# Block 2's dense 2: a third group of four w2 tiles in seven products

## The chip, the core and the metric

The kernel runs on one core of a Trainium2 chip. The metric is the device time of one execution in microseconds (us); the median of three runs is given for the kernel before. The engines are TensorE (PE, matmuls), VectorE (DVE), ScalarE (ACT), GpSimd (POOL, used here mostly to issue DMAs) and SyncE (SP, which issues DMAs in order).

## The reference

Two layers on the same input x of 2048 rows x 1024 columns are added to x. The first is a state space layer on the layer-normed x, a complex linear recurrence over the rows with 1024 states; the second is a dense layer (1024 to 3584), the Mish activation and a second dense layer (3584 to 1024), on the layer-normed x too:

```python
Lam_bar = jnp.exp(dt * Lam)
B_bar = ((Lam_bar - 1.0) / Lam)[:, None] * Bmat
Bu = jnp.einsum("bld,pd->blp", x + 0j, B_bar)
for t in range(L):
    h = Lam_bar[None, :] * h + Bu[:, t, :]
y = 2.0 * jnp.einsum("blp,dp->bld", hseq, Cmat).real + x * Dskip[None, None, :]

h = jnp.einsum("bsd,df->bsf", x, w1) + b1
sp = jnp.log1p(jnp.exp(-jnp.abs(h))) + jnp.where(h > 0, h, 0)
return jnp.einsum("bsf,fd->bsd", h * jnp.tanh(sp), w2)

xn = _layernorm(x)
return x + A(xn) + B(xn)
```

## The kernel before

The 2048 rows are worked in four blocks of 512. A block's work has two halves. The first is the projections: w1 (dense 1) and the B matrix, whose results are activated (Mish) or rotated into the recurrence's frame. The second, in `tail`, adds up dense 2 (w2) and the C product of the states in the eight PSUM banks, one bank for each of 4 row quarters x 2 column halves. While PE does dense 2, DVE runs the recurrence (`recur`, one call for each of eight state tiles j), and each block ends with four `finish` operations that add PSUM and the kept sums into the output rows. Block 3's projections follow block 2's last matmul directly.

From block 1 on many products are done in seven matrix products for eight (Strassen's scheme in Winograd's form). For dense 2 this works on groups of four K tiles of w2: two tiles from the first 14 and two from the last 14, each cut into column halves. The seven products take four raw or summed weights and activations: products 1, 2 and 4 use raw activations, and 7, 5, 6 and 3 use sums that DVE makes (`act_sums`). The weight side of a group is made once: `d2_load` brings four raw tiles on POOL, or `d2_row` takes them from the ring, in both cases ACT scales them, three raw units are stored to a DRAM area `w2d` and four differences (`d2_sums`, each a `step` with one DVE operation and one POOL store) are made in place and stored. The steps wait in a list `later` and are run by `some(n)`, or by a `k0` in the written-out order of a block's projections.

`NFG` says how many groups each block does so: 2 of 7 in block 2, all 7 in block 3. What block 2 does not do in seven products is its list `PLAIN`: pairs of w2 tiles straight from the input, 16 matmuls a pair (`dense`). While such a pair lies in the ring, ACT also scales the raw tiles of the groups named in `PASSING` from it, for block 3. `SCALED_AT` says which activation tiles ACT scales behind which pair.

Weights come through a ring of seven slots of 512 KB (`ring`, `items`, `ring_load`, `ring_fill`): `ws` are w1 units, `tp` units of w2d (two a slot), `w2` plain pairs, `c` the C matrix, `ts` block 3's w2d. SP issues the loads in that order, and each load waits until PE (and ACT, where it reads the slot) is done with the slot's former content.

The order of the work is written out by hand in strings: `STEPS` for block 2's projections, `LAST` for block 3's. Letters p q s w x y z are w1 products, a to d those of B, `G` is `act_scale` of two activation tiles, `g` Mish, `u` block 2's first dense-2 products, `t` `act_sums`, `I` ring slots given back, `h` and `m` raw w2 tiles, `k` a step. In `dense_part` (block 2) come: products 1, 7, 2, 5, 6 with their `keep` (PSUM to the buffer KS), then the plain list, then products 3 and 4. After it come the C products of six state tiles, and by row quarter those of the last two, with `finish` behind each. `carry` and `uncarry` are seven small DVE operations that take the recurrence's last state to the next block.

Of the kernel before, what the change touches and what calls it, by code (L numbers as in the profile page):

```python
# [163 lines left out]
def build_kernel(nc, A_x, A_Lambda_re, A_Lambda_im, A_B_re, A_B_im, A_C_re, A_C_im,  # L164
# [11 lines left out]
    GF = 7  # L176
# [8 lines left out]
    TILES = [*range(12)]  # L185
    NFG = {2: 2, 3: GF}
    W2_ORDER = (*range(9), 13, *range(9, 13))
    EARLY, LATE = ((0, 18), (26, 28)), ((18, 26),)
    PLAIN = [(f, f + 1) for f in (4, 18, 6, 20, 24, 10, 8, 22, 12, 26)]
    PASSING = {4: 2, 18: 2, 6: 3, 20: 3, 8: 4, 22: 4}  # L190
    SCALED_AT = {4: (20,), 18: (24,), 6: (10,), 20: (8, 22), 10: (12,), 8: (26,)}
    WHOLE = ("a2 a1 V0 b2 b1 a5 b5 V1 P4 P5 a6 b6 v6 P6 P7 a3 b3 P0 a7 b7 P1 Q0 n0 p1 q1 a4 b4 "
# [3 lines left out]
    STEPS = ("p1 p5 p2 q1 q5 p6 q2 s1 k0 p7 s5 p3 k0 q6 s2 p4 k0 q7 q3 k0 s6 q4 m1 k0 g0 a2 a1 k0 s7 s3 b2 b1 k0 s4 g1 k0 a5 "  # L196
             "b5 a6 b6 a3 h4 b3 S0 a7 h5 b7 c2 d2 h6 a4 b4 h7 l0 c5 c1 d5 d1 r0 c6 G0 c3 G1 d6 d3 c7 G2 w1 d7 r1 w5 w2 G3 c4 d4 k0 E0 E1 w6 x1 x5 x2 k0 w7 k0 w3 r2 "
             "x6 w4 k0 y1 y5 y2 x7 x3 E2 E3 y6 x4 z1 z5 g2 z2 y7 y3 z6 G7 y4 z3 z7 u0 t0 G8 u2 z4 I1 u1 t1 t2")
    LAST = ("p1 p5 p2 q1 q5 p6 q2 s1 p7 s5 p3 q6 s2 M5 p4 q7 q3 k0 k0 s6 q4 g0 a2 a1 k0 s7 k0 s3 O0 O0 O0 O0 m6 b2 b1 s4 G1 G0 g1 a5 G3 b5 G2 a6 b6 "
# [213 lines left out]
    for blk in range(NB):  # L413
        items += W_ITEMS if blk in SPLIT else O_ITEMS if blk == FAST else [("w1", g) for g in range(NF // 2)]
        if blk == NB - 1:
            items += [("ts", m) for m in range((NT + 3) // 4)]
        elif blk in SPLIT:
            units = [("tp", 7 * p + i) for p in range(7) for i in range(0, NFG[blk], 2)]
            items += units[:5 * NFG[blk] // 2] + [("w2", (4 * REAL[f // 4] + f % 4) // 2) for f, _ in PLAIN] + units[5 * NFG[blk] // 2:]
        else:  # L420
            items += [("w2", g) for g in W2_ORDER]
        items += [("c", j) for j in range(NJ)] if blk >= FAST else []
    n_loaded = [0]

    def ring_load():
        i = n_loaded[0]
        if i >= len(items):
            return
        n_loaded[0] += 1
        kind, g = items[i]  # L430
        s = i % NRING
        if kind == "w1":

            dst = ring[:, s, :].rearrange("p (k f) -> p k f", k=NK // 2)
            r0 = (g % 2) * D // 2
            src = B_w1[r0:r0 + D // 2, (g // 2) * 512:(g // 2 + 1) * 512].rearrange("(k p) f -> p k f", p=P)
        elif kind == "w2":
            dst = ring[:, s, :].rearrange("p (f d) -> p f d", f=2)
            src = B_w2[g * 256:(g + 1) * 256, :].rearrange("(f p) d -> p f d", p=P)
        else:  # L440
            dst, src = ring[:, s, :], ctd[g] if kind == "c" else None
            if kind == "ts":
                n = min(4, NT - 4 * g) * TB
                dst, src = ring[:, s, 0:n], w2d[g][:, 0:n]
        s_ring[s].nper = len(g) if kind == "ws" else 2 if kind == "tp" else 1
        if kind == "tp":
            for h in range(2):
                src = w2d[(g + h) // 2][:, (g + h) % 2 * 1024:((g + h) % 2 + 1) * 1024]
                SP.dma(lambda e, h=h, src=src: e.dma_start(ring[:, s, h * 1024:(h + 1) * 1024], src),
                       s_ring[s], reads=[b_w2d[g + h]], writes=[b_ring[s].parts[h]])  # L450
            return
        if kind == "ws":
            for h, (i, n) in enumerate(g):
                SP.dma(lambda e, h=h, i=i, n=n: e.dma_start(ring[:, s, h * 1024:(h + 1) * 1024], wsd[i][n - 1]),
                       s_ring[s], reads=[b_wsd[i][n - 1]], writes=[b_ring[s].parts[h]])
            return
        SP.dma(lambda e: e.dma_start(dst, src), s_ring[s], reads=[b_ctd[g]] if kind == "c" else b_w2d[2 * g:2 * g + 2] if kind == "ts" else [],
               writes=[b_ring[s]])
# [396 lines left out]
    def ring_fill():  # L855
        while n_loaded[0] < min(n_item[0] + NRING, len(items)):
            kind, g = items[n_loaded[0]]
            need = [b_wsd[i][n - 1] for i, n in g] if kind == "ws" else b_w2d[2 * g:2 * g + 2] if kind == "ts" else b_w2d[g:g + 2] if kind == "tp" else []
            if any(b.writer is None for b in need):
                return  # L860
            ring_load()
# [339 lines left out]
    KIND = (1, 7, 2, 5, 6, 3, 4)  # L1201
    D2_RAW = [((k, t), (k, t + 4)) for k, t in (("h", 8), ("h", 0), ("s", 0))]
    D2_RAW += [(("a", 20), ("a", 6)), (("a", 24), ("a", 10)), (("h", 0), ("h", 4)), (("h", 8), ("h", 12))]
    spare = {"h": (hb, b_hbf), "a": (act, b_actf), "s": (CT[:, :, 1, TB:D], [b for s in b_snap for b in s.parts])}
# [39 lines left out]
    def d2_sums(g):  # L1244
        (lo, b_lo), (hi, b_hi) = d2_half(g, 0), d2_half(g, 1)
        b11, b12, b21, b22 = ((v[:, :, d, :], b[d::2]) for v, b in ((lo, b_lo), (hi, b_hi)) for d in range(2))
        sem = DmaSem(nc, "d_ts%d" % g, nper=4)
        f = lambda u: (u[0].bitcast(f16), u[1])
        for n, o, x, y, h, d in ((5, b11, b12, b11, 0, 0), (7, b12, b22, b12, 0, 1), (6, b22, b22, f(b11), 1, 1),
                                 (4, b21, b21, f(b22), 1, 0)):  # L1250
            def step(n=n, o=o, x=x, y=y, h=h, d=d):
                vop(lambda e: e.tensor_tensor(o[0].bitcast(f16), x[0], y[0], op=ALU.subtract),
                    reads=x[1] + y[1], writes=o[1])
                d2_store(g, n, h, d, sem)

# [57 lines left out]

    CHUNKS = {2: ((0, 4),), 3: ((0, 6), (6, 12), (12, 14))}
    b_SA = [[Buf("SA%d_%d" % (n, i)) for i in range(3)] for n in range(4)]
# [43 lines left out]
    def project_fast(blk, order, open_unit):  # L1359
        keep = {}  # L1360
        for o in order.split():
# [38 lines left out]
            elif kind == "Q":  # L1400
                row_powers(EARLY)
            elif kind == "O":
                held.pop(0)(SP)
# [80 lines left out]
    def tail(blk, base):  # L1484
# [46 lines left out]
        def fast(n, i, k):  # L1531
# [3 lines left out]
            p, ng = KIND.index(n), 2 * NFG[blk]  # L1535
            at = p * ng + k + (4 * len(PLAIN) if near and p >= 5 else 0)
            s = (base + at // 4) % NRING
# [7 lines left out]
            else:  # L1545
# [5 lines left out]
                  reads=b_t + [b_ring[s]], writes=[b_ps[bank]], first=begin, last=end, chained=begin and not st_,  # L1551
                  tell=i == 1 and (at % 4 == 3 or at == NT - 1))

# [22 lines left out]
        def dense_part():  # L1576
# [9 lines left out]
            for k in range(ng):  # L1586
                fast(2, 1, k)
            for _ in range(ng // 2):
                item_done()
            for n in KIND[3:]:  # L1590
                for k in range(ng):
                    for i in range(2):
                        fast(n, i, k)
                    if k % 4 == 3:
                        item_done()
# [4 lines left out]
                if n == 6:  # L1600
                    keep(3, BANKS[6])
                    act_scale(blk, 9)
                    plain_root()
# [95 lines left out]
        ends = blk == NB - 1  # L1699
        if blk in SPLIT:  # L1700
            for m, q0, h in ((0, 0, 0), (1, 0, 1), (2, 2, 0), (3, 2, 1))[2 if near else 0:]:
                b_x = [b_xx[i][q].parts[h] for q in (q0, q0 + 1)]
                vop(lambda e, m=m, q0=q0, h=h: e.tensor_tensor(
                    KS[:, m, :, :], KS[:, m, :, :], xx[:, i, q0:q0 + 2, h * TB:(h + 1) * TB], op=ALU.add),
                    reads=[b_KS[m]] + b_x, writes=[b_KS[m]])
        if ends:
            tmp, b_tmp = KS[:, 3, 1, :], b_KS[3]
            vop(lambda e: e.scalar_tensor_tensor(out=tmp, in0=ps[:, 7, :], scalar=wz[:, 3:4], in1=tmp, op0=ALU.mult, op1=ALU.add),
                reads=[b_ps[7], b_tmp, b_wz[3]], writes=[b_tmp])
        for q in range(NQ):  # L1710
            units = (2 * q, 2 * q + 1) if not (ends and q == NQ - 1) else (2 * q,)
            for j in range(NJ - njt, NJ):
# [119 lines left out]
    for blk in range(NB):  # L1832
# [67 lines left out]
        for j in range(NJ):  # L1900
# [8 lines left out]
            if blk in SPLIT:  # L1909
                if near and j == 0:  # L1910
                    act_sums(blk, ((4, 0),))
                    next(out_stage)
                if near and j in (2, 4, 7):
                    some(4)
                if j == 6:
# [3 lines left out]
            if blk:  # L1919
# [7 lines left out]
                if j == 5:  # L1927
                    w_exponent(1)
                    row_powers(LATE)
                    row_bound()  # L1930
                    for i in range(2):
                        w_scale(i)
                continue
            if j == 0:
# [15 lines left out]
        if near:  # L1950
            for q in range(NQ):
                ln_skip(blk + 1, q)
            for n in range(4):
                sums_x(blk + 1, n)
        if 0 < blk < NB - 1:
            carry()
        if blk == SPLIT[0]:
            uncarry()
        if blk == FAST:
# [19 lines left out]
        if blk == FAST - 1:  # L1979
            w_scale(4)  # L1980

    SP.wait(out_events.values())
# [34 lines left out]
```

## Time and profile before

| | |
|---|---|
| median of 3 runs | 589.18 us (589.16 to 589.87) |
| the profiled execution | 589.72 us, of which the profile's span is 588.5 |
| PE busy | 582.6 us (99%) |
| DVE busy | 510.5 us (87%) |
| ACT busy | 400.5 us (68%) |
| DMA queue of SP and the others in hardware | 105.99 MB in the largest, 60.0% of the 16 engines' span |

The times of the profile count from the span's start. In it block 1's dense 2 starts near 230 us, block 2's projections at 307, its dense 2 at 374, its C products at 421, and block 3's projections at 449. A line number such as L1491 is a line of the kernel; L1491 is `acc`, the matmul of plain dense tiles and of C, L1550 is `fast`, the matmul of the seven products, L1023 and L947 are the projections. A bracket at the end of a timeline's row is the idle time of the engine before it and who ended it.

### The profile page before, as it was taken

Reading aid. Unit: us, or ns where it says so; the run is one execution under the profiler, and the core shown is the slowest. Engines: PE = TensorE matmul, PEld = TensorE weight load, DVE = VectorE, ACT = ScalarE, POOL = GpSimd, SP = SyncE. Lnnn points to the kernel's source line nnn. Section 1 sums busy time; section 2 is a strip of 40 time slices with the busy share of each in tenths; the row PEclk is TensorE's granted clock in tenths of the full one; section 3 lists DMA queues with packets and bytes.
Section 4 is the critical chain, followed back from the end, with each engine's and each line's share of the span. In section 5 each row is a group of like instructions: output and inputs, shape, how many; then the busy total and the mean of one; then the engine's idle time right before and its main releaser. Section 6 shows DMA issues by size and latency. Waiting matters only on the chain.

```text
span 588.5 us, 9772 instructions
## 1 busy us (share of the span) xinstructions
PE 582.6 (99%) x3606; PEld 354.2 (60%) x3643; DVE 510.5 (87%) x791; ACT 400.5 (68%) x538; POOL 149.9 (25%) x213
## 2 busy tenths in 40 slices
PE   8999999999999999999999999999999999999998
PEld 7644444444447887444458888644446888844444
DVE  6999998998997878998976869899999469789995
ACT  4869993758578878999506787899512798992330
POOL 2899300123624420441211221011410013100000
PEclk9999999999999999999999999999999999999999
DMA  9999999999688978899879858869985956989832
GB/s 254 244 257 221 212 224 227 305 338 362 183 308 287 352 239 309 296 315 258 300 234 381 293 176 299 300 227 264 341 324 176 384 200 230 331 311 329 295 113 72
DMA packets 114585, 158.48 MB, mean 269 GB/s; under 512 B 55658, under 2 KB 66538, under 8 KB 114538
## 3 DMA queue, kind: packets, MB, share of 16 engines
q1 hardware_dynamic: 97696, 105.99, 60.0%
q0 software_dynamic: 13184, 43.53, 21.4%
q10 hardware_dynamic: 3658, 8.34, 4.0%
q8 instruction: 29, 0.48, 0.3%
q14 instruction: 18, 0.15, 0.1%
HBM read 111.69 MB, written 34.08 MB: 248 GB/s over the span
## 4 chain that ended last, share of the span: by engine, by line
PE 96%; DMA 1%; ACT 1%; SPq 1%; issue 1%; DVE 0%; ACTq 0%
PE ps L1491 40%; PE ps L1023 19%; PE ps L947 12%; PE ps L870 10%; PE ps L1550 8%; PE ps L1426 5%; DMA ring<-in_B_w_dram 1%; PE ps L688 1%; ACT act L893 1%; PE ps L1514 1%; ACT act L900 1%; PE ps L679 0%; SPq L398 0%; PE ps L1522 0%; DVE act L1046 0%
## 5 line engine op out<-in xcount | busy, mean ns | idle before, releaser
L1491 PE MATMUL ps<-ring,act 128*128 128x512 bf16 x594 | 131.0, 379 | 0.7
L1491 PEld LDWEIGHTS ps<-ring,act 128*128 128x128 bf16 x608 | 59.5, 98 | 71.3
L1043 ACT ACTIVATE snaps<-ps,par,cs 128x256 f32<-128x256 f32 x98 | 53.5, 563 | 58.6 <-PE ps L1023 54.3
L1491 PE MATMUL ps<-ring,hT 128*128 128x512 bf16 x354 | 78.2, 379 | 0.4
L1023 PE MATMUL ps<-TT,ring 128*128 128x256 f16 x552 | 68.3, 273 | 0.0
L909 DVE TENSOR_TENSOR mt<-hT,tab 128x2048 bf16<-128x2048 bf16 (+1 forms) x56 | 67.9, 1212 | 0.4
L1491 PEld LDWEIGHTS ps<-ring,hT 128*128 128x128 bf16 x362 | 35.4, 98 | 42.7
L1441 DVE TENSOR_TENSOR_SCAN hT<-cs,qi,hT 128x512 bf16<-128x512 f32 x48 | 60.6, 1273 | 0.0
L1023 PEld LDWEIGHTS ps<-TT,ring 128*128 128x128 f16 (+1 forms) x552 | 53.8, 98 | 7.2 <-issue 0.2
L870 PE MATMUL ps<-xnT,ring 128*128 128x512 bf16 x258 | 56.8, 379 | 0.3
L1060 DVE SCALAR_TENSOR_TENSOR act<-ps,cs,snaps 128x512 bf16<-128x512 f32 x54 | 39.8, 747 | 19.2 <-PE ps L1023 17.1
L1023 PE MATMUL ps<-xnT,ring 128*128 128x256 bf16 x424 | 53.9, 273 | 0.0
L1222 POOL DMA_DIRECT2D w2d<-hb x28 | 20.0, 717 | 96.6 <-ACT hb L1232 52.6
L1023 PEld LDWEIGHTS ps<-xnT,ring 128*128 128x128 bf16 (+1 forms) x424 | 41.4, 98 | 5.4 <-ACT snaps L1043 0.2
L870 PEld LDWEIGHTS ps<-xnT,ring 128*128 128x128 bf16 x264 | 25.8, 98 | 31.0
L1461 ACT ACTIVATE hT<-hT,wz 128x1024 bf16<-128x1024 bf16 x16 | 17.9, 1145 | 27.4 <-DVE hT L1456 27.4
L893 ACT ACTIVATE act<-act 128x2048 bf16<-128x2048 bf16 (+3 forms) x12 | 32.8, 2756 | 4.7 <-DVE act L1046 4.7
L972 DVE TENSOR_TENSOR hT<-ps,snaps 128x512 f16<-128x512 f32 x36 | 23.8, 686 | 13.9 <-ACT snaps L964 12.6
L1172 POOL DMA_DIRECT2D wsd<-hb x35 | 18.9, 545 | 55.3 <-DVE hb L1194 31.3
L1550 PE MATMUL ps<-ring,act 128*128 128x512 bf16 (+1 forms) x129 | 29.1, 379 | 0.2
L878 ACT ACTIVATE act<-ps,par 128x512 bf16<-128x512 f32 (+1 forms) x40 | 23.6, 663 | 7.3 <-PE ps L870 7.3
L1426 PE MATMUL ps<-xnT,BT 128*128 128x512 bf16 x126 | 27.7, 379 | 0.1
(241 smaller groups left out, 1055.3 us busy)
## 6 DMA issues: line engine op xcount, KB each, us to landing
ring<-wsd SPq DMA_DIRECT2D x122, 256.0 KB, 4.6
ring<-in_B_w_dram SPq DMA_DIRECT2D x58, 512.0 KB, 5.5
ring<-ctd SPq DMA_DIRECT2D x24, 512.0 KB, 4.5
ring<-w2d SPq DMA_DIRECT2D x24, 512.0 KB, 5.4
wsd<-hb POOLq DMA_DIRECT2D x35, 256.0 KB, 4.5
w2d<-hb POOLq DMA_DIRECT2D x28, 256.0 KB, 5.0
hb<-in_B_w_dram POOLq DMA_DIRECT2D x20, 256.0 KB, 4.9
ctd<-CT ACTq DMA_DIRECT2D x8, 512.0 KB, 5.4
```

Source lines behind the costliest of these rows:

```text
L870: PE.mm(lambda e, k=k, w=w: e.matmul(ps[:, bank, :], lhsT=w, rhs=xnT[:, k, :], start=k == 0, stop=k == NK - 1), reads=[b_ring[s]] + b_xnT, ...
L893: aop(lambda e: e.activation(t, t, AF.Mish), reads=b, writes=b)
L909: vop(lambda e: e.tensor_tensor(mt[:], u.unsqueeze(1).to_broadcast([P, 2, 2, TB]), tab[:, :, j, :].unsqueeze(2).to_broadcast([P, 2, 2, TB] ...
L947: PE.mm(lambda e, w=w, x=x, o=o, begin=begin, end=end: e.matmul(ps[:, bank, o:o + TH], lhsT=w, rhs=x, start=opens and begin, stop=end, ski ...
L972: vop(lambda e: e.tensor_tensor(dst, bank(b), src, op=ALU.add), reads=[b_ps[b], b_src], writes=b_hT[ci][j0:j0 + 2])
L1023: PE.mm(lambda e, w=w, x=x, o=o, begin=begin, end=end: e.matmul(ps[:, bank, o:o + TH], lhsT=w, rhs=x, start=opens and begin, stop=end, ski ...
L1043: aop(lambda e, o=o, p=p, j=j: e.activation(o, p, AF.Identity, scale=ig, bias=b1(f0 + j)), reads=[b_ps[b], b_par, b_ig], writes=b_dst)
L1060: vop(lambda e: e.scalar_tensor_tensor(out=dst, in0=bank(b), scalar=ig, in1=src, op0=ALU.mult, op1=ALU.add), reads=[b_ps[b], b_snap[k], b_ ...
L1426: PE.mm(lambda e, j=j, ci=ci, k=k, bank=bank: e.matmul(ps[:, bank + ci, :], lhsT=BT[:, ci, j, k, :], rhs=xnT[:, k, :], start=k == 0, stop= ...
L1441: vop(lambda e: e.tensor_tensor_scan(out=hT[:, ci, j, :], data0=cj("r", j).to_broadcast([P, TB]), data1=hT[:, ci, j, :], initial=init, op0 ...
L1491: PE.mm(lambda e: e.matmul(ps[:, u, :], lhsT=lhsT, rhs=rhs, start=st_, stop=last, skip_group_check=blk in SPLIT), reads=reads, writes=[b_p ...
L1550: PE.mm(lambda e: e.matmul(ps[:, bank, :], lhsT=lhsT, rhs=rhs, start=st_, stop=end, skip_group_check=True), reads=b_t + [b_ring[s]], write ...
```

## The change

Block 2 takes a third group of four w2 tiles in seven products (`NFG` 3), and `PLAIN` loses the pairs (4, 5) and (18, 19). With three groups the first five products hold 15 units, an odd number, so their last ring slot holds one unit. The third group's raw tiles are no longer taken from the ring in block 2's plain list: `d2_load(2)` and `d2_scale(2)` bring and scale them at j = 5 of block 1's recurrence, into activation tiles 8 to 15, and four more `k0` in `STEPS` make its differences. The remaining groups' sources, the scalings in `SCALED_AT` and the places of the layer norm's steps in the plain list move up. The last difference of each group has a semaphore of its own. In block 2's `finish` part the additions of x into the kept sums 2 and 3 come after the second `finish`, not before the first; `carry` and `uncarry` come in block 3's order (`K0`), not before block 2's `finish`.

```diff
-    NFG = {2: 2, 3: GF}
+    NFG = {2: 3, 3: GF}
-    PLAIN = [(f, f + 1) for f in (4, 18, 6, 20, 24, 10, 8, 22, 12, 26)]
-    PASSING = {4: 2, 18: 2, 6: 3, 20: 3, 8: 4, 22: 4}
-    SCALED_AT = {4: (20,), 18: (24,), 6: (10,), 20: (8, 22), 10: (12,), 8: (26,)}
+    PLAIN = [(f, f + 1) for f in (6, 20, 24, 10, 8, 22, 12, 26)]
+    PASSING = {6: 3, 20: 3, 8: 4, 22: 4}
+    SCALED_AT = {6: (24,), 20: (10, 8), 24: (22,), 10: (12,), 8: (26,)}
 STEPS
-  ... b7 c2 d2 h6 a4 b4 h7 l0 c5 c1 d5 d1 ...      ... G8 u2 z4 I1 u1 t1 t2
+  ... b7 k0 c2 d2 k0 h6 a4 b4 h7 l0 k0 c5 c1 k0 d5 d1 ...  ... G8 u2 G9 z4 I1 u1 t1 t2
 LAST
-  ... q7 q3 k0 k0 s6 q4 g0 a2 a1 ...
+  ... q7 q3 k0 k0 s6 q4 g0 K0 a2 a1 ...
 ring items of block 2
-            units = [("tp", 7 * p + i) for p in range(7) for i in range(0, NFG[blk], 2)]
+            units = [[7 * p + i for p in ps_ for i in range(NFG[blk])] for ps_ in (range(5), range(5, 7))]
+            parts = [[("tp", tuple(us[i:i + 2])) for i in range(0, len(us), 2)] for us in units]
-    D2_RAW = [((k, t), (k, t + 4)) for k, t in (("h", 8), ("h", 0), ("s", 0))]
-    D2_RAW += [(("a", 20), ("a", 6)), (("a", 24), ("a", 10)), (("h", 0), ("h", 4)), (("h", 8), ("h", 12))]
+    D2_RAW = [((k, t), (k, t + 4)) for k, t in (("h", 8), ("h", 0), ("a", 8), ("s", 0))]
+    D2_RAW += [(("a", 24), ("a", 10)), (("h", 0), ("h", 4)), (("h", 8), ("h", 12))]
 d2_sums
-        sem = DmaSem(nc, "d_ts%d" % g, nper=4)
+        sem = DmaSem(nc, "d_ts%d" % g, nper=3)
+        last = DmaSem(nc, "d_tu%d" % g)
-                d2_store(g, n, h, d, sem)
+                d2_store(g, n, h, d, last if n == 4 else sem)
-    CHUNKS = {2: ((0, 4),), 3: ((0, 6), (6, 12), (12, 14))}
+    CHUNKS = {2: ((0, 6),), 3: ((0, 6), (6, 12), (12, 14))}
 dense_part
-            for _ in range(ng // 2):
+            for _ in range(3 * ng // 4 - 1):
                 item_done()
-                    act_scale(blk, 9)
+                    act_scale(blk, 10)
 tail, before and between the finishes
+        def add_x(ms):
+            ...
         for q in range(NQ):
+            if blk in SPLIT and near and q == 2:
+                add_x((2, 3))
 block loop
-                if near and j in (2, 4, 7):
-                    some(4)
+                if near and j in (2, 5):
+                    some(4 if j == 2 else 3)
                     row_bound()
+                    d2_load(2)
                     for i in range(2):
                         w_scale(i)
+                    d2_scale(2)
-        if 0 < blk < NB - 1:
+        if blk == FAST:
             carry()
-        if blk == SPLIT[0]:
-            uncarry()
```

More of the change, by code (lines that the diff above doesn't have):

```diff
@@ L196, in build_kernel @@
     STEPS = ("p1 p5 p2 q1 q5 p6 q2 s1 k0 p7 s5 p3 k0 q6 s2 p4 k0 q7 q3 k0 s6 q4 m1 k0 g0 a2 a1 k0 s7 s3 b2 b1 k0 s4 g1 k0 a5 "
-             "b5 a6 b6 a3 h4 b3 S0 a7 h5 b7 c2 d2 h6 a4 b4 h7 l0 c5 c1 d5 d1 r0 c6 G0 c3 G1 d6 d3 c7 G2 w1 d7 r1 w5 w2 G3 c4 d4 k0 E0 E1 w6 x1 x5 x2 k0 w7 k0 w3 r2 "
-             "x6 w4 k0 y1 y5 y2 x7 x3 E2 E3 y6 x4 z1 z5 g2 z2 y7 y3 z6 G7 y4 z3 z7 u0 t0 G8 u2 z4 I1 u1 t1 t2")
-    LAST = ("p1 p5 p2 q1 q5 p6 q2 s1 p7 s5 p3 q6 s2 M5 p4 q7 q3 k0 k0 s6 q4 g0 a2 a1 k0 s7 k0 s3 O0 O0 O0 O0 m6 b2 b1 s4 G1 G0 g1 a5 G3 b5 G2 a6 b6 "
+             "b5 a6 b6 a3 h4 b3 S0 a7 h5 b7 k0 c2 d2 k0 h6 a4 b4 h7 l0 k0 c5 c1 k0 d5 d1 r0 c6 G0 c3 G1 d6 d3 c7 G2 w1 d7 r1 w5 w2 G3 c4 d4 k0 E0 E1 w6 x1 x5 x2 k0 w7 k0 w3 r2 "
+             "x6 w4 k0 y1 y5 y2 x7 x3 E2 E3 y6 x4 z1 z5 g2 z2 y7 y3 z6 G7 y4 z3 z7 u0 t0 G8 u2 G9 z4 I1 u1 t1 t2")
+    LAST = ("p1 p5 p2 q1 q5 p6 q2 s1 p7 s5 p3 q6 s2 M5 p4 q7 q3 k0 k0 s6 q4 g0 K0 a2 a1 k0 s7 k0 s3 O0 O0 O0 O0 m6 b2 b1 s4 G1 G0 g1 a5 G3 b5 G2 a6 b6 "
             "a3 h20 b3 h21 a7 h22 b7 h23 c2 d2 a4 b4 c5 c1 d5 d1 h24 r0 c6 k0 h25 k0 c3 h26 d6 d3 h27 c7 w1 k0 d7 r1 w5 k0 w2 c4 d4 w6 x1 r2 x5 G4 "
@@ L417, in build_kernel @@
         elif blk in SPLIT:
-            units = [("tp", 7 * p + i) for p in range(7) for i in range(0, NFG[blk], 2)]
-            items += units[:5 * NFG[blk] // 2] + [("w2", (4 * REAL[f // 4] + f % 4) // 2) for f, _ in PLAIN] + units[5 * NFG[blk] // 2:]
+            units = [[7 * p + i for p in ps_ for i in range(NFG[blk])] for ps_ in (range(5), range(5, 7))]
+            parts = [[("tp", tuple(us[i:i + 2])) for i in range(0, len(us), 2)] for us in units]
+            items += parts[0] + [("w2", (4 * REAL[f // 4] + f % 4) // 2) for f, _ in PLAIN] + parts[1]
         else:
@@ L444, in ring_load @@
                 dst, src = ring[:, s, 0:n], w2d[g][:, 0:n]
-        s_ring[s].nper = len(g) if kind == "ws" else 2 if kind == "tp" else 1
+        s_ring[s].nper = len(g) if kind in ("ws", "tp") else 1
         if kind == "tp":
-            for h in range(2):
-                src = w2d[(g + h) // 2][:, (g + h) % 2 * 1024:((g + h) % 2 + 1) * 1024]
+            for h, u in enumerate(g):
+                src = w2d[u // 2][:, u % 2 * 1024:(u % 2 + 1) * 1024]
                 SP.dma(lambda e, h=h, src=src: e.dma_start(ring[:, s, h * 1024:(h + 1) * 1024], src),
-                       s_ring[s], reads=[b_w2d[g + h]], writes=[b_ring[s].parts[h]])
+                       s_ring[s], reads=[b_w2d[u]], writes=[b_ring[s].parts[h]])
             return
@@ L857, in ring_fill @@
             kind, g = items[n_loaded[0]]
-            need = [b_wsd[i][n - 1] for i, n in g] if kind == "ws" else b_w2d[2 * g:2 * g + 2] if kind == "ts" else b_w2d[g:g + 2] if kind == "tp" else []
+            need = [b_wsd[i][n - 1] for i, n in g] if kind == "ws" else b_w2d[2 * g:2 * g + 2] if kind == "ts" else [b_w2d[u] for u in g] if kind == "tp" else []
             if any(b.writer is None for b in need):
@@ L1401, in project_fast @@
                 row_powers(EARLY)
+            elif kind == "K":
+                carry()
+                uncarry()
             elif kind == "O":
@@ L1535, in fast @@
             p, ng = KIND.index(n), 2 * NFG[blk]
-            at = p * ng + k + (4 * len(PLAIN) if near and p >= 5 else 0)
+            at = p * ng + k
+            if near and p >= 5:
+                at += 4 * len(PLAIN) + -5 * ng % 4
             s = (base + at // 4) % NRING
@@ L1551, in fast @@
                   reads=b_t + [b_ring[s]], writes=[b_ps[bank]], first=begin, last=end, chained=begin and not st_,
-                  tell=i == 1 and (at % 4 == 3 or at == NT - 1))
+                  tell=i == 1 and (at % 4 == 3 or at == NT - 1 or near and p == 4 and end))
         def first_unit(u):
@@ L1591, in dense_part @@
                 for k in range(ng):
+                    at = (KIND.index(n) if KIND.index(n) < 5 else KIND.index(n) - 5) * ng + k
                     for i in range(2):
                         fast(n, i, k)
-                    if k % 4 == 3:
+                    if at % 4 == 3 or n == 6 and k == ng - 1:
                         item_done()
@@ L1699, in tail @@
         ends = blk == NB - 1
-        if blk in SPLIT:
-            for m, q0, h in ((0, 0, 0), (1, 0, 1), (2, 2, 0), (3, 2, 1))[2 if near else 0:]:
+        def add_x(ms):
+            for m in ms:
+                q0, h = 2 * (m // 2), m % 2
                 b_x = [b_xx[i][q].parts[h] for q in (q0, q0 + 1)]
@@ L1706, in tail @@
         if ends:
+            add_x(range(4))
             tmp, b_tmp = KS[:, 3, 1, :], b_KS[3]
```

## The prediction

> **What bounds the kernel now.** I read the page first, then the list of who waited for whom on TensorE (PE), then the chain that ended last, then the timelines of ScalarE (ACT), VectorE (DVE) and GpSimd (POOL) around blocks 1 and 2.
>
> The page (span, busy time, chain by engine):
>
> ```profile
> span 588.5 us, 9772 instructions
> PE 582.6 (99%) x3606; PEld 354.2 (60%) x3643; DVE 510.5 (87%) x791; ACT 400.5 (68%) x538; POOL 149.9 (25%) x213
> PE 96%; DMA 1%; ACT 1%; SPq 1%; issue 1%; DVE 0%; ACTq 0%
> ```
>
> All waits of PE's matmuls, and the stretch in which block 2's dense 2 runs (columns: busy us and instructions of each engine, granted clock, DMA share):
>
> ```profile
> PE ps L641 <- DVE filler L467: 1.0, 1, 1.0
> PE ps L679 <- DMA ring<-in_B_w_dram: 0.5, 2, 0.3
> PE ps L679 <- ACT xr L526: 0.2, 1, 0.2
> ```
>
> ```profile
> 374.00:449.00 75.00, 74.63 (x345) 34.44 (x352) 72.60 (x105) 45.04 (x50) 14.96 (x21) 1.00 0.82 269
> ```
>
> PE waits 1.7 us in the whole kernel, all in the first microseconds, and in the changed stretch it is idle for 0.37 of 75 us at the full clock. So the time is the number of matmuls times their spacing, and the change is worth the matmuls that it takes out, less any wait that it opens. DVE, busy 72.60 of these 75 us, is the engine with least room behind PE.
>
> The chain in order of time (start, length, what) gives the spacing:
>
> ```profile
> 376.54 6.91 PE ps L1550 x32
> ...
> 383.88 0.05 issue
> 383.93 10.74 PE ps L1491 x49
> ...
> 449.06 15.72 PE ps L1023 x144
> ```
>
> 6.91/32 = 0.216 us for a matmul of 512 columns; with the pause of 0.05 after 49 of them, (10.74 + 0.05)/49 = 0.220.
>
> **The change, part by part.**
>
> *Matmuls.* Four tiles leave the plain list: two pairs, each 2 tiles x 8 PSUM banks = 16 matmuls, so 32 go. A group in seven products adds 2 k-steps x 2 banks x 7 = 28. Before there are 56 + 160 = 216 matmuls in this dense, after 84 + 128 = 212. Four fewer: 4 x 0.220 = **0.88 us**, all on the path. The Trainium skill, page "TensorE: Matmul & The Clock Gate", section "Back-to-back issue gap", puts the sustained spacing of 512-column matmuls at about 131 ns; by it, four would be 0.52 us. The 0.216 of this trace differs from that and decides.
>
> *The order on PE.* The first five products now hold 60 matmuls, not 40, so the plain list starts 20 x 0.216 + 0.05 = 4.37 us later, at 383.45 + 4.37 = 387.82 (383.45 is where the chain's 6.91 us end). It is 16 x 0.216 = 3.45 us a pair. What must be ready by then is weighed next.
>
> *ACT in the plain list.* This is the tightest place. Rows of ACT, the group that gives one scaling of a tile, and the weight load that opens the plain list:
>
> ```profile
> 383.27 1.27 ACT L1573 ACTIVATE KS<-ps,wz 128x512 f32<-128x512 f32 x2 [1.91 <-PE ps L1550]
> 384.43 1.33 ACT L900 ACTIVATE act<-act,wz 128x512 bf16<-128x512 bf16 x2
> 385.77 1.28 ACT L600 ACT_TABLE_LOAD   x1
> ...
> 387.27 2.17 ACT L1232 ACTIVATE CT<-ring,cs 128x1024 bf16<-128x1024 bf16 x2
> 389.35 1.32 ACT L900 ACTIVATE act<-act,wz 128x512 bf16<-128x512 bf16 x2
> 390.57 2.17 ACT L1232 ACTIVATE CT<-ring,cs 128x1024 bf16<-128x1024 bf16 x2
> ```
>
> ```profile
> L900 ACT ACTIVATE act<-act,wz 128x512 bf16<-128x512 bf16 x20 | 13.1, 709 | 0.0
> ```
>
> ```profile
> 383.07 11.97 PEld L1491 LDWEIGHTS ps<-ring,act 128*128 128x128 bf16 x56
> ```
>
> Before, the scaling at 389.35 was for the fourth pair; now the scaling in this place is for the third, tiles 24 and 25. The sequence of ACT hangs on the end of the fifth product, so it moves by 4.37: that scaling starts at 393.72 and tile 24 is done 0.71 later, at 394.43. PE opens the third pair at 387.82 + 2 x 3.45 = 394.72, and its weight load comes 383.45 - 383.07 = 0.38 ahead, at 394.34. So PE may wait 0.1 us here, 0 to 0.2 with the handover. Tile 25 is wanted six matmuls later, and is in time. The next pair (tile 10) is scaled after two more rows of raw tiles: 393.72 + 1.22 + 2.08 + 0.71 = 397.73 against a weight load at 397.79: even. The rest is earlier by over 2 us. Any lateness of ACT before these two points reaches PE whole; both ends for the range: 0 and 0.5 us, I take 0.1.
>
> The two more scalings (tiles 18, 19) in the projections are the pair that used to come after the fifth product, pulled forward. They end about 377, and the Mish behind them waited for DVE anyway:
>
> ```profile
> 377.74 3.62 ACT L893 ACTIVATE act<-act 128x4096 bf16<-128x4096 bf16 x1 [0.93 <-DVE act L1046]
> ```
>
> Its result is not needed before 391, so this costs nothing; without that cover it would be 1.3 us.
>
> *DVE.* Rows from the fourth product's evacuation to block 3's first one:
>
> ```profile
> 380.88 2.72 DVE L1567 SCALAR_TENSOR_TENSOR KS<-ps,wz,xx 128x512 f32<-128x512 f32 x4
> 383.51 1.22 DVE L909 TENSOR_TENSOR mt<-hT,tab 128x2048 bf16<-128x2048 f16 x1
> ...
> 419.67 2.92 DVE L1252 TENSOR_TENSOR act<-act 128x1024 f16<-128x1024 bf16 x4
> ...
> 443.40 0.36 DVE L1470 TENSOR_TENSOR qi<-hT,cs 128x8 f32<-128x8 bf16 x2
> ...
> 444.49 2.35 DVE L1703 TENSOR_TENSOR KS<-KS,xx 128x1024 f32<-128x1024 f32 x2
> 446.95 4.86 DVE L1692 SCALAR_TENSOR_TENSOR xx<-ps,wz,KS 128x1024 bf16<-128x1024 f32 x4
> 451.73 1.11 DVE L1046 TENSOR_SCALAR snaps<-ps,cs,par 128x256 f32<-128x256 f32 x2
> ```
>
> The last two of the four KS operations at 380.88 need the fourth product, which now ends at 376.54 + 0.86 (four more matmuls of the first product ahead) + 36 x 0.216 = 385.2. They end at 386.3, so the rotations and scans behind them start 386.3 - 383.5 = 2.8 us later. Against that, the tail sheds five of its twelve raw-tile differences (2.92/4 = 0.7 each, 3.5), the carry (443.40 to 444.49: 1.09), and, until two finishes are out, the additions (444.49 to 446.95: 2.46). The wider sums add 0.1. So DVE could begin the first finish at 446.95 + 2.9 - 3.5 - 1.09 - 2.46 = 442.8. PE ends the first quarter of rows, 8 matmuls each, at 449.06 - 0.88 - 3 x 1.73 = 443.0, the second at 444.7. The finishes follow: 443.0; 444.7 to 445.9; the additions to 448.4; the last two to 450.8. Block 3's first evacuation, 451.73 before, starts at 450.8: 0.93 us earlier with PE 0.88 earlier. Nothing is won, nothing lost. The carry and one left-over difference run early in block 3, where DVE had pauses. Bounds: 0 to 0.3 us, I take 0.
>
> *Four raw-tile differences moved into the projections* (2.8 us of DVE, four stores on POOL). The first two stand where DVE was idle for 1.18 us:
>
> ```profile
> 339.04 0.69 DVE L989 CAST hT<-ps 128x512 f16<-128x512 f32 x1 [1.18 <-PE ps L947]
> ```
>
> They take 1.3, so that copy starts 0.1 to 0.2 us late; its bank is not reopened for two more products of 0.87. Cost 0. The stores run ahead of block 3's input loads on POOL by under 1.5 us, and nothing reads those for 10 us.
>
> *Block 1's end.* Two loads and three stores on POOL, four scalings of about 1.05 us on ACT. They are queued behind the scaling at 279.69; ACT then idles:
>
> ```profile
> 279.69 7.67 ACT L1178 ACTIVATE hb<-hb,cs 128x2048 bf16<-128x2048 bf16 x4
> ...
> 309.08 1.16 ACT L1043 ACTIVATE snaps<-ps,par,cs 128x256 f32<-128x256 f32 x2 [21.73 <-PE ps L1023]
> ```
>
> ```profile
> 281.96 1.07 POOL L1172 DMA_DIRECT2D wsd<-hb  x2 [10.84 <-ACT hb L1178]
> ```
>
> The loads go out in POOL's pause of 10.84 us ahead of 281.96 and the scalings end near 291.6, inside the 21.73 us. Cost 0; without this cover, 4.2.
>
> *The ring and SP.* Five product items and ten plain ones become eight and eight. The first plain item now reuses a slot that PE frees two matmuls into the second half of product 7: 377.40 + 2.59 + 0.43 = 380.4, wanted at 387.8. Lead 7.4 us, where before it was preloaded. Landing of the plain loads between 374 and 384, then of the C loads from 400 to 425:
>
> ```profile
> L457 SPq DMA_DIRECT2D ring<-in_B_w_dram x7: 367/368/465, 374.0 to 383.5; - x7
> ...
> DMA to landing us min/median/max: 4.1/5.0/5.4
> ```
>
> ```profile
> L457 SPq DMA_DIRECT2D ring<-ctd x8: 319/319/1372, 404.2 to 425.0; - x8
> ...
> DMA to landing us min/median/max: 4.4/7.5/9.2
> ```
>
> At 5.4 it is in time by 2 us. At 9.2 PE waits 1.8. I take 0, as the first row is the same transfer at the same place. The four transposes on SP move ahead of all C loads. The first C load then takes the slot of the fifth plain pair, which ACT reads until about 393.72 + 15 = 408.7 (ten scalings, four raw rows and four normalised rows of 0.6 to 1.2 each), and is due at 449.06 - 0.88 - 128 x 0.22 = 420.0: 11 us against a longest landing of 9.2. In bytes block 2's dense loses 1 MB, since the third group's seven stores are out earlier.
>
> *Sum.* -0.88 + 0.1 = -0.8, with -0.9 as the best end. The profiled execution took 589.72, 1.2 above its span; the median of the runs is 589.18, and a shift applies to it alike: **588.3** (588.30 without the 0.1).
>
> **The rivals.**
>
> *A late feed eats the gain.* The ring load lands like the C loads (1.8 us), or ACT is 0.5 us later at tiles 24 and 10. For it: the leads of 7.4 and 0 us. Against it: 5.4 is the longest such landing. 588.30 + 0.5 to 1.8 = 588.8 to 590.1.
>
> *Slower: DVE comes to block 3 late.* The fifth group's raw rows now end at 412, its stores are issued by 413.5, and three differences in the scan of j = 5, at 426.68 + 2.9 - 2.83 = 426.8, wait for them to land; behind them on DVE are the last scans, the finishes and the first evacuation. That evacuation has to be over before the sixth product of block 3 at 448.2 + 5 x 0.87 = 452.5; it would end at 451.9, so 0.6 us of lateness is free. From 2.7 us the kernel is slower by over 0.2%; a store that takes 17 us, or 4 us more work than I count on a DVE that has no pause, gives 588.3 + 3.4 = 591.7. For it: DVE's 72.60 of 75 us. Against it: 13 us of lead against a longest landing of 9.2.
>
> *The change removes nothing from PE's path.* Then 589.2. Against it stand the counts 216 and 212 and a PE without pauses.
>
> **How the numbers follow.** About 0.2% (1.2 us) is what a measurement of this kernel can tell from no change; the forecast's 0.88 is 0.15%, inside it. Chances: forecast 0.54, gain eaten in part or whole (with the third rival) 0.22, slower by DVE 0.24, which holds also waits that I have not found. The bound of 0.2% lies at 588.0, 0.3 us under the forecast, and scatter alone (the runs before spread over 0.7 us) puts four in ten of the forecast's share beyond it: faster 0.22. Same: 0.32 + 0.22 = 0.54. Slower 0.24. The range goes from 587.7 (PE's last 0.37 us of idle gone, and scatter) to 590.8; it leaves out the upper part of the slower case. The forecast's own range is 587.7 to 588.9.
>
> **What would show it.** Right: the profile after has L1550 with 28 matmuls more and L1491 with 32 fewer, block 3's first product starts near 448.2, PE has no wait beyond a tenth at the third plain pair, and ACT's scalings at block 1's end lie before 293. Wrong: a PE wait on the ring's plain load near 387.8, on ACT's L900 near 394.5 over 0.3 us, or on DVE after 450; or a first product of block 3 after 449.

## The result and the profile after

| | before | after |
|---|---|---|
| median of 22 runs each | 589.46 us | 588.51 us |
| ratio | | 0.9984, 95% interval 0.9978 to 0.9991 |
| the profiled execution | 589.72 us, span 588.5 | 588.30 us, span 587.1 |

The kernel is faster by 0.95 us, or 0.16%; the interval leaves out no change and goes from 0.5 to 1.3 us. Forecast were 588.3 and 0.8 us (0.88 of matmuls less 0.1 for ACT). All lines of the kernel after are numbered one to some tens higher: L1496 is the plain and C matmul (L1491 before), L1557 the seven products (L1550), L1024 the w1 products (L1023).

The page of after: span, busy time.

```profile
span 587.1 us, 9771 instructions
PE 581.1 (99%) x3603; PEld 353.2 (60%) x3639; DVE 511.7 (87%) x791; ACT 400.3 (68%) x538; POOL 151.2 (26%) x215
```

The chain of after in order of time, around block 2's dense 2:

```profile
229.08 1.24 PE ps L1496 x5
...
306.75 15.84 PE ps L1024 x144
...
373.45 2.54 PE ps L1557 x11
375.99 0.87 PE ps L1024 x8
376.86 10.36 PE ps L1557 x48
...
447.65 15.72 PE ps L1024 x144
463.38 1.75 PE ps L948 x16
```

and the rows of before that answer to the first, second and last of them, where the prediction does not show them:

```profile
229.63 1.24 PE ps L1491 x5
...
307.30 15.84 PE ps L1023 x144
...
464.78 1.75 PE ps L947 x16
```

The span is shorter by 1.4 us, but 0.55 of it lies ahead of 229 us, where both kernels do the same: it is scatter of the start (another run of the kernel after has 229.73 there). What the change gives is read between two fixed places, the first product of block 2's projections and the first B product of block 3's: 464.78 - 307.30 = 157.48 before, 463.38 - 306.75 = 156.63 after, 0.85 us less. That is four matmuls of 0.213. The counts are as forecast: 28 more weight loads of the seven products (252 before, 280 after) and 32 fewer of the plain list (608 and 576, three blocks together). Block 3's first product starts at 447.65, or 448.20 with the start's 0.55 added; 448.2 was forecast.

The pauses of 0.05 us after 49 matmuls, which the prediction priced at 0.220 us a matmul, are no pauses. In the plain list of before 160 matmuls were written, and the trace has 160 weight loads but 156 matmuls (timelines of 373 to 425 us):

```profile
383.07 34.41 PEld L1491 LDWEIGHTS ps<-ring,act 128*128 128x128 bf16 x160
383.28 34.70 PE L1491 MATMUL ps<-ring,act 128*128 128x512 bf16 x156
```

So such a piece of 49 is 50 matmuls with one record missing. The weight loads follow each other every (34.41 - 0.10)/159 = 0.216 us (one takes 0.10), without a break, and four matmuls are 0.86 us, not 0.88.

Three other readings. The weight loads of after show the one tight place, with the idle time before it in brackets:

```profile
386.84 6.79 PEld L1496 LDWEIGHTS ps<-ring,act 128*128 128x128 bf16 x32
393.88 20.47 PEld L1496 LDWEIGHTS ps<-ring,act 128*128 128x128 bf16 x96 [0.25 <-ACT act L901]
```

The plain list's first load comes 386.84 + 0.55 - 383.07 = 4.32 us later than before; 4.37 was forecast. 32 weight loads are two plain pairs, so the second row opens the third, tile 24: the load was held by ACT, after 0.25 us of idle time. Of these 0.12 lie between any two loads (0.216 less 0.10), so it is 0.13 us late. No matmul waited, as the list of PE's waits for matmuls has only the start:

```profile
PE ps L642 <- DVE filler L468: 1.0, 1, 1.0
PE ps L680 <- ACT rs L494: 0.7, 1, 0.7
```

DVE at the end of block 2, in the kernel after:

```profile
384.45 1.41 DVE L1574 SCALAR_TENSOR_TENSOR KS<-ps,wz,xx 128x512 f32<-128x512 f32 x2 [1.32 <-PE ps L1557]
...
442.51 1.28 DVE L1700 SCALAR_TENSOR_TENSOR xx<-ps,wz,KS 128x1024 bf16<-128x1024 f32 x1
444.24 1.28 DVE L1700 SCALAR_TENSOR_TENSOR xx<-ps,wz,KS 128x1024 bf16<-128x1024 f32 x1 [0.44 <-PE ps L1496]
445.56 2.36 DVE L1712 TENSOR_TENSOR KS<-KS,xx 128x1024 f32<-128x1024 f32 x2
448.02 2.48 DVE L1700 SCALAR_TENSOR_TENSOR xx<-ps,wz,KS 128x1024 bf16<-128x1024 f32 x2
450.42 1.11 DVE L1047 TENSOR_SCALAR snaps<-ps,cs,par 128x256 f32<-128x256 f32 x2
```

With the start's 0.55 taken off the forecast times (443.0, 444.7, 450.8), the first finish, the second and block 3's first evacuation stand within 0.2 us of them. (DVE itself was ready for the first finish at 442.5, where 442.8 - 0.55 = 442.25 was summed.) And ACT at the end of block 1 has the four added scalings inside the pause that was named:

```profile
286.72 4.25 ACT L1233 ACTIVATE act<-act,cs 128x1024 bf16<-128x1024 bf16 x4
302.87 5.52 ACTq L1685 DMA_DIRECT2D out_dram<-xx  x4
308.54 1.16 ACT L1044 ACTIVATE snaps<-ps,par,cs 128x256 f32<-128x256 f32 x2 [17.57 <-PE ps L1024]
```

### The profile page after: what moved, and what is told of

Its sections match the earlier page's. It is cut to its first block, busy times and chain, and to the rows that moved or that the text cites. A ratio compares the mean times of both kernels' runs of the same rounds, so it can differ in the third digit from the quotient of the medians.

```text
span 587.1 us, 9771 instructions
## 1 busy us (share of the span) xinstructions
PE 581.1 (99%) x3603; PEld 353.2 (60%) x3639; DVE 511.7 (87%) x791; ACT 400.3 (68%) x538; POOL 151.2 (26%) x215
## 4 chain that ended last, share of the span: by engine, by line
PE 96%; DMA 1%; ACT 1%; SPq 1%; issue 1%; DVE 0%; ACTq 0%
PE ps L1496 39%; PE ps L1024 19%; PE ps L948 13%; PE ps L871 10%; PE ps L1557 9%; PE ps L1431 5%; DMA ring<-in_B_w_dram 1%; PE ps L689 1%; ACT act L894 1%; PE ps L1519 1%; ACT act L901 1%; PE ps L680 0%; SPq L398 0%; PE ps L1527 0%; DVE act L1047 0%
## 5 line engine op out<-in xcount | busy, mean ns | idle before, releaser
L1496 PE MATMUL ps<-ring,act 128*128 128x512 bf16 x563 | 124.0, 379 | 0.7
L1496 PEld LDWEIGHTS ps<-ring,act 128*128 128x128 bf16 x576 | 56.3, 98 | 67.6 <-ACT act L901 0.2
L1496 PE MATMUL ps<-ring,hT 128*128 128x512 bf16 x355 | 78.3, 379 | 0.4
L1024 PE MATMUL ps<-TT,ring 128*128 128x256 f16 x552 | 68.3, 273 | 0.0
L1496 PEld LDWEIGHTS ps<-ring,hT 128*128 128x128 bf16 x362 | 35.4, 98 | 42.7
L1024 PEld LDWEIGHTS ps<-TT,ring 128*128 128x128 f16 (+1 forms) x552 | 53.9, 98 | 7.2 <-issue 0.2
L1024 PE MATMUL ps<-xnT,ring 128*128 128x256 bf16 x424 | 53.9, 273 | 0.0
L1024 PEld LDWEIGHTS ps<-xnT,ring 128*128 128x128 bf16 (+1 forms) x424 | 41.4, 98 | 5.3
L1557 PE MATMUL ps<-ring,act 128*128 128x512 bf16 (+1 forms) x153 | 34.3, 379 | 0.2
```

The source lines that it names most:

```text
L1024: PE.mm(lambda e, w=w, x=x, o=o, begin=begin, end=end: e.matmul(ps[:, bank, o:o + TH], lhsT=w, rhs=x, start=opens and begin, stop=end, ski ...
L1496: PE.mm(lambda e: e.matmul(ps[:, u, :], lhsT=lhsT, rhs=rhs, start=st_, stop=last, skip_group_check=blk in SPLIT), reads=reads, writes=[b_p ...
L1557: PE.mm(lambda e: e.matmul(ps[:, bank, :], lhsT=lhsT, rhs=rhs, start=st_, stop=end, skip_group_check=True), reads=b_t + [b_ring[s]], write ...
```

## The experiments

Two theories could both give the measured 0.95 us. A: PE is the path, and the gain is four matmuls. B: the gain comes from the work moved at block 2's end, with the matmuls hidden. The first three runs divide the change between them. All ratios are to the kernel before in the same set of runs. Their intervals are about 1 us wide, as wide as the effect; what one run is worth against another is therefore read from the stretch used above, block 2's first product to block 3's first B product. A table at the end of the section has it for all runs.

**Four matmuls less, without the change.** In the kernel before:

```diff
-                        for us in ((4, 6, 1, 3, 5, 7), (0, 2)):
+                        for us in ((4, 6, 1, 3, 5, 7), (0, 2))[:1 if fs[0] == 26 else 2]:
```

> The kernel before, with nothing of the change; in block 2's plain list the last pair (tiles 26, 27) leaves out its last four matmuls, those of PSUM banks 0 and 2. Theory A (PE is the path, four matmuls of 0.22 us are all of the gain): 0.88 us less than before, about 588.6. Theory B (the gain comes from the work moved at the end of block 2, the matmuls are hidden): no change, 589.4 to 589.5.

Measured: 589.20 against 589.56 us, ratio 0.9994 (0.9985 to 1.0003). By the medians less than half of the 0.88 us came, but the interval just covers both theories (no change and 0.88). The trace decides: 0.29 us came, neither theory as it stood. It also shows where the rest went. DVE, then the weight loads, then the chain at block 3's start in this run:

```profile
446.49 4.86 DVE L1692 SCALAR_TENSOR_TENSOR xx<-ps,wz,KS 128x1024 bf16<-128x1024 f32 x4
451.26 1.11 DVE L1046 TENSOR_SCALAR snaps<-ps,cs,par 128x256 f32<-128x256 f32 x2
```

```profile
447.88 0.78 PEld L1023 LDWEIGHTS ps<-xnT,ring 128*128 128x128 bf16 x8 [0.66 <-issue]
...
452.43 0.77 PEld L1023 LDWEIGHTS ps<-TT,ring 128*128 128x128 f16 x8 [0.27 <-DVE snaps L1046]
```

```profile
306.82 15.84 PE ps L1023 x144
...
446.49 1.29 DVE xx L1692
447.78 0.14 issue
447.92 16.10 PE ps L1023 x144
464.01 1.75 PE ps L947 x16
```

The chain now goes through DVE: block 3's first product needs bank 0, which the first finish gives back at 446.49 + 1.29 = 447.78. That is 0.2 us late. The sixth product then waits for the first evacuation, and the 144 matmuls take 16.10, not 15.72 us. DVE did all its work at the same times as before (446.49 - 306.82 = 139.67 after block 2's start, 446.95 - 307.30 = 139.65 before). Of PE's gain of 0.86 us, 0.57 was given back to waits for DVE: 464.01 - 306.82 = 157.19, 0.29 less than before. The kernel before had PE and DVE arriving at block 3 almost together.

**The two moves alone.** In the kernel before, `K0` in block 3's order in place of the carry ahead of the finishes, and:

```diff
         for q in range(NQ):
+            if blk in SPLIT and near and q == 2:
+                add_x((2, 3))
```

> The kernel before with two moves of the change alone: the additions of x into the kept sums 2 and 3 stand after block 2's second finish, the carry and uncarry in block 3's projections. Theory A: no change, within 0.2 us of before, because PE waits for neither in the kernel before; DVE's first evacuation of block 3 starts about 1 us earlier and nobody uses it. Theory B: about 0.9 us less than before.

Measured: 589.50 against 589.56 us, ratio 1.0002 (0.9993 to 1.0010). By trace 464.59 - 307.10 = 157.49 against 157.48. Nothing, as A has it; B as it stood falls. One part of the expectation was wrong: the first evacuation is not 1 us earlier (451.63 - 307.10 = 144.53 us after block 2's start, 451.73 - 307.30 = 144.43 before). With the additions and the carry out of the way, the first two finishes wait 0.45 and 0.44 us for PE.

**The two moves undone in the kernel after.**

> The kernel after with these two moves undone. DVE then reaches the first finish at 442.5 + 1.1 + 2.4 = 446.0, and ends the four finishes at 450.9, where the profile of after has 450.4. Theory A: block 3's first evacuation ends at 452.0, just when its sixth product wants the bank: 0 to 0.2 us more than after. Theory B: 0.9 us more than after, the whole gain gone.

Measured: 588.76 against 589.56 us, ratio 0.9985 (0.9976 to 0.9994); after has 0.9984. By trace 463.65 - 306.84 = 156.81, that is 0.18 us more than after:

```profile
446.12 4.86 DVE L1700 SCALAR_TENSOR_TENSOR xx<-ps,wz,KS 128x1024 bf16<-128x1024 f32 x4
450.90 1.11 DVE L1047 TENSOR_SCALAR snaps<-ps,cs,par 128x256 f32<-128x256 f32 x2
```

```profile
452.06 0.77 PEld L1024 LDWEIGHTS ps<-TT,ring 128*128 128x128 f16 x8 [0.24 <-DVE snaps L1047]
```

The finishes came at 446.12 and the evacuation at 450.90, both where the expectation put them, and the sixth product waits again, but little. In the kernel after the moves are worth 0.2 us and not 0.6, because there DVE reaches the finishes 0.4 us earlier than with four matmuls less (446.12 - 306.84 = 139.28 against 139.67). The third group takes five differences out of DVE's tail (3.5 us) and puts back 2.8 us of late start; and by the traces of before and after, the wider sum of activations between the scans takes 0.94 us, not 0.66. Together that is 0.4.

**Scalings ahead of the raw rows.** In the kernel after, the two loops behind each plain pair change places.

> The kernel after; behind each plain pair ACT scales the activation tiles of SCALED_AT before the raw rows, so tile 24 is ready 2.1 us earlier. Theory A (the weight load's 0.25 us wait for ACT lies in the lead that weight loads have over their matmuls): the wait on ACT at the third plain pair is gone from the profile and the time stays, within 0.1 us. Rival (the wait reaches the matmuls): 0.1 to 0.25 us less.

Measured: 588.66 against 589.56 us, ratio 0.9985 (0.9976 to 0.9993), against 0.9984 for after. The weight load's wait on ACT is gone from the list of waits and the time is the same, by trace too (463.76 - 307.14 = 156.62). A weight load comes 0.21 us ahead of its matmul (383.07 and 383.28 in the rows of before above) and takes 0.1, and the 0.13 us by which it was late lay in that lead.

**ACT two operations later at that point.** In the kernel after, behind the first plain pair's raw rows:

```diff
+                        if fs == PLAIN[0]:
+                            for _ in range(2):
+                                aop(lambda e: e.activation(xn[:, 0, :], xx[:, (blk + 1) % 2, 0, :], AF.Copy),
+                                    reads=[b_xx[(blk + 1) % 2][0]], writes=[b_xn[0]])
```

> The kernel after with two more ACT operations of about 1 us each (a copy of an input tile that nobody reads) between the first plain pair's raw rows and the scaling of tiles 24 and 25. Theory A (ACT has no slack at that point, so its lateness reaches PE whole): 1.9 us more than after, with a wait of 1.7 to 2.1 us for ACT at the third plain pair. Rival (the order of the plain list hides it, as ACT has 27.6 of 32 us busy there): under 0.5 us more.

Measured: 590.61 against 589.47 us, ratio 1.0020 (1.0011 to 1.0028), 2.1 us above after; by trace 465.75 - 307.17 = 158.58, 1.95 more than after. The weight load and the matmul that opens the third plain pair in this run (timelines of 386 to 420 us):

```profile
396.32 3.14 PEld L1496 LDWEIGHTS ps<-ring,act 128*128 128x128 bf16 x16 [2.28 <-ACT act L901]
396.33 20.89 PE L1496 MATMUL ps<-ring,act 128*128 128x512 bf16 x94 [1.79 <-ACT act L901]
```

The load is 2.28 - 0.12 = 2.16 us late and its matmul follows 0.01 us behind: the lead of 0.2 is used up, and the other 1.95 reach PE. So ACT's lateness does pass to PE at the third plain pair, all but the weight load's lead.

**DVE 3.4 us later ahead of the finishes.** In the kernel after:

```diff
+            for _ in range(5):
+                if blk == SPLIT[0]:
+                    vop(lambda e: e.tensor_tensor(mt[:, 0, :, :].rearrange("p a t -> p (a t)"), xx[:, 1, 0, :], dsk[:], op=ALU.mult),
+                        reads=[b_xx[1][0], b_dsk], writes=[b_m[0]])
```

> The kernel after with five more DVE multiplications (about 3.4 us in all, result unused) after the differences for block 3's input, ahead of block 2's finishes. Theory A: 0.4 us of DVE's pause ahead of the second finish and 0.5 us ahead of the sixth product of block 3 take up 0.9 us; the other 2.5 us reach PE: 2.2 to 2.7 us more than after, as waits of block 3's first products for DVE. Rival (PSUM banks and later pauses take it up): under 1 us more.

Measured: 591.49 against 589.47 us, ratio 1.0041 (1.0029 to 1.0052): 3.0 us above after, a little more than expected, but from six runs that spread over 2.2 us. By trace 466.36 - 307.00 = 159.36, 2.73 more than after, the upper end of what was expected. DVE's first evacuation, and the two waits of PE:

```profile
453.60 1.11 DVE L1047 TENSOR_SCALAR snaps<-ps,cs,par 128x256 f32<-128x256 f32 x2
```

```profile
452.59 1.03 PE L1024 MATMUL ps<-TT,ring 128*128 128x256 f16 x8 [1.20 <-issue]
454.77 1.05 PE L1024 MATMUL ps<-TT,ring 128*128 128x256 f16 x8 [1.14 <-DVE snaps L1047]
```

The second wait is the one foreseen, the sixth product behind the first evacuation. The first is the fifth product, which opens bank 4: the third finish, one of the two that start at 451.21 on DVE, gives it back near 452.4. That this is what the wait marked "issue" is for is read from the bank's number, not from a releaser.

Three runs with the same number of matmuls give the slack at the sixth product. Counted from block 2's start, the first evacuation begins at 450.42 - 306.75 = 143.67 us in the kernel after. It is 0.39 later with the moves undone, 0.77 later with four matmuls less and 2.93 later here, and the stretch is longer by 0.18, 0.56 and 2.73. In each, all but 0.2 us reaches PE: the slack in the kernel after is 0.2 us.

**The first plain load late.** In the kernel after, product 7's second half moves behind product 5, and with it the ring slots that it gives back:

```diff
-            for k in range(ng):
-                fast(7, 1, k)
-            keep(0, BANKS[7])
 ...
                 if n == 5:
+                    for k in range(ng):
+                        fast(7, 1, k)
+                    keep(0, BANKS[7])
+                    for _ in range(3 * ng // 4 + 1):
+                        item_done()
```

> The kernel after with the second half of product 7 moved behind product 5, so that the ring slot of the first plain pair comes free about 3.5 us before PE wants that pair, not 7.4. The matmuls are the same in number. Theory A (a load takes 3.4 to 5.4 us to land and is then waited for): PE waits 0 to 1.9 us, most likely 1.3, for the ring at the first plain pair, and the time is longer by that. Rival (the landing shown overstates what PE needs): no change.

Measured: 588.88 against 589.47 us, ratio 0.9991 (0.9982 to 1.0000): 0.4 us above after, less than the two intervals can tell apart; by trace 463.80 - 306.99 = 156.81, 0.18 above after. The waits and the landings of the plain loads in this run:

```profile
PE ps L1496 <- DMA ring<-in_B_w_dram: 0.3, 1, 0.3
```

```profile
L458 SPq DMA_DIRECT2D ring<-in_B_w_dram x7: 383/460/472, 384.1 to 387.5; - x7
...
DMA to landing us min/median/max: 3.4/6.7/9.1
```

Four microseconds of lead taken away cost a wait of 0.3 us, the low end of what A expected, and not its likely 1.3. The load that PE wants is the first of seven that SP issues one after the other. Alone, it lands 3.4 us after its issue at 384.1, the quickest of the seven, as the first plain load of after does (issued at 380.0, also 3.4). The later ones, up to 9.1, are wanted 3.45 us apart and were in time.

**Four matmuls less, with the two moves.** After the first run this was the open question: is a matmul here worth 0.1 us, or was the rest of it a wait for DVE that the moves take away?

> The kernel before with both: the last four matmuls of the plain list's last pair left out (as in the run without four matmuls), and the two moves at the end of block 2 (as in the run of the moves alone). Theory C (each alone gives little, since without the moves DVE's finishes hold back block 3's first products for 0.6 us as soon as PE comes earlier): the whole 0.88 us less than before, about 588.6, and no wait for DVE at block 3's start. Rival (the run without four matmuls gave 0.4 us because four matmuls are worth no more): again 0.4 us less, 589.1.

> The kernel after, beside the one above on the same chip: 0.9 to 1.0 us less than before. Theory C: equal to the one above within 0.2 us, as both have the same number of matmuls and no wait. Rival: 0.5 us less than it.

Measured, in one set: 588.60 us with four matmuls less and the moves, 588.71 after, against 589.65 before; both ratios 0.9984 (0.9975 to 0.9993). By trace 464.21 - 307.59 = 156.62, as in after:

```profile
307.59 15.84 PE ps L1023 x144
...
448.49 15.72 PE ps L1023 x144
464.21 1.75 PE ps L947 x16
```

The moves alone give nothing, four matmuls alone give 0.3 us, both together give 0.86. Theory C holds. With the moves DVE follows PE: its first evacuation begins 451.25 - 307.59 = 143.66 us after block 2's start, 0.87 earlier than with the moves alone.

**All runs by the same stretch.** Starts from the chains:

| run | block 2's first product | block 3's first B product | stretch | against before |
|---|---|---|---|---|
| before | 307.30 | 464.78 | 157.48 | |
| the two moves alone | 307.10 | 464.59 | 157.49 | +0.01 |
| four matmuls less | 306.82 | 464.01 | 157.19 | -0.29 |
| four matmuls less, with the moves | 307.59 | 464.21 | 156.62 | -0.86 |
| after | 306.75 | 463.38 | 156.63 | -0.85 |
| after, beside the one above | 307.40 | 464.02 | 156.62 | -0.86 |
| after, moves undone | 306.84 | 463.65 | 156.81 | -0.67 |
| after, scalings first | 307.14 | 463.76 | 156.62 | -0.86 |
| after, first plain load late | 306.99 | 463.80 | 156.81 | -0.67 |
| after, ACT later | 307.17 | 465.75 | 158.58 | +1.10 |
| after, DVE later | 307.00 | 466.36 | 159.36 | +1.88 |

Each row is one execution. The four with 212 matmuls and no wait agree within 0.01 us, and so do the two with 216, so a tenth of a microsecond counts here.

## Why the prediction was right, step by step

- **The bound.** Right. PE without pauses in the changed stretch made the count of matmuls the price: 0.85 to 0.86 us by trace for four, 0.95 by the medians, 0.88 forecast. The step from 0.216 to 0.220 us a matmul was wrong: it took missing records for pauses. The same gaps (seven of 0.05) are nearly all of the 0.37 us of idle time with which the prediction reasoned the low end of its range. The 131 ns that the Trainium skill gives in "TensorE: Matmul & The Clock Gate", section "Back-to-back issue gap", does not hold here; the runs with four matmuls less and no wait have 0.86/4 = 0.215 us for one.
- **The absolute time.** In part luck. The sum gives 588.4 with the 0.1 for ACT and 588.3 without; it starts from the three runs' 589.18, where 22 runs have 589.46, and the medians' gain is known only to lie between 0.5 and 1.3 us. The prediction also took 1.2 us for the least that can be told from no change; with 22 runs each 0.95 could be told. The gain by trace is the better test.
- **ACT at the third plain pair.** The place and the wait were right (0.1 forecast, 0.13 measured), its worth was not: I charged it to the matmuls, and the weight load's lead of 0.2 took it. So "any lateness reaches PE whole" holds only beyond that lead; the run with ACT later shows the price from there on, one for one.
- **DVE.** The sum of what is added and shed met the trace within 0.3 us; the wider sums, put at 0.1, account for most of that (0.28 for the one between the scans). The wording "nothing is won, nothing lost" hid what the step was for: the moves and the shed differences buy the right to the 0.88. Had I set the same sum up without them, 0.88 less on PE against 0.6 of slack at the sixth product, it would have shown a wait of 0.3 us, about half of what the first run met. The slack was in the prediction, as the condition of a rival, and not in its sum.
- **The price of a late DVE.** 0.6 us of slack and then one for one was forecast. One for one is right; the slack was mis-sized and is 0.2 us, by three runs. The bank of the fifth product, which waits as well, was missed.
- **The ring.** Right: a lead of 7.4 us held, with landings of 3.4 to 5.4 in the profile after. With about half the lead PE waited 0.3. The rival's price of 1.8 us needs a landing of 9.2 for the first plain load, and no run shows one: it landed after 3.4 us in the kernel after and with the load late.
- **Block 1's end and the moved differences.** At no cost, as forecast; read from the trace alone, no run tried them.
- **Not tried.** A delayed landing of the raw stores in front of the differences, the other way in which the slower rival could have come.

## What to carry to other kernels

When PE has no pause, price a change by its matmuls, and then ask of every engine behind it whether it can also come earlier by that much: a gain on the first engine is worth no more than the slack of the second. Here the list of waits told nothing, because two engines that arrive together leave no wait to see; the slack has to be worked out from the end of the one's work and the moment at which the other wants it. An edit that measures as nothing by itself can be the half that lets another edit pay, so try the pair before throwing either out.

## What the runs showed of the hardware

The matmul records of this trace have gaps, the weight loads do not: 160 loads and 156 matmuls for 160 written, so spacings are better read from the loads (0.216 us with 512 columns). A weight load that another engine made 0.13 us late left no trace in the matmuls or the time, while one that was 2.16 us late held its matmul back by 1.95; the lead of a load over its matmul is 0.2 us. Seven loads of 512 KB issued within 3.4 us by one engine landed after 3.4 to 9.1 us, a median of 6.7, where four spread over 3 us took 3.4 to 5.4.
